# Two attention and feed-forward layers: seven-product blocks start one feature group later, and their sums are spread over plain units

## The chip, the cores and the metric

The kernel runs on one core of a Trainium2 chip. The core has five engines with queues of their own: TensorE (PE in the profile; its weight loads are listed as PEld), VectorE (DVE), ScalarE (ACT), GpSimd (POOL) and SyncE (SP, which here only issues DMA transfers). The metric is the device time of one execution in microseconds, lower is better. The time before is the median of three runs, 2001.54 us (2000.5 to 2002.94).

## The reference

The input is x with 2048 rows of 448 numbers in 32-bit float. Two layers with the same weights are applied; each is an attention stage and a feed-forward stage, both on a normalized copy of x and both added to x:

```python
x = x + _A_ref(_layernorm(x), A_wq, A_wk, A_wv, A_wo)   # 16 heads of 28, one shared key and value head
x = x + _B_ref(_layernorm(x), B_w_gate, B_w_up, B_w_down)
# and the same two lines once more

def _B_ref(x, w_gate, w_up, w_down):
    g = _silu(x @ w_gate)          # 448 x 1792
    u = x @ w_up                   # 448 x 1792
    return (g * u) @ w_down        # 1792 x 448
```

Only the feed-forward stages are touched by the change.

## The kernel before

**Precision.** Every matrix operand is split into a high part and a rest (`h` and `l` in names, by `split` on GpSimd: a rounding copy at line 139 and a subtraction at line 140), and a product is the sum of three: high by high, high by rest, rest by high.

**Tiling of the feed-forward stage.** The 2048 rows of x are four chunks of 512. The 1792 features are 14 slices of 128, here called features 0 to 13, and taken in seven groups of two (FG = 2), groups 0 to 6. The 448 inputs are three slices of 128 and one of 64; the last is held twice, in both halves of the partitions. All matrix products of the stage are issued in pairs, one on the lower 64 rows of the array and one on the upper 64 (`side_by_side`, line 338), so that two run side by side.

**Plain units.** `unit(group, chunk, n)` does one feature for one chunk: gate and up products into two of four low PSUM banks (42 products in 21 pairs), silu on ScalarE (line 1092), the product with up on VectorE (1093), rounding on ScalarE (1094), the rest on VectorE (1097). The down products of a unit (24 in 12 pairs, into four high banks) are kept in a list, `pend`, and are issued inside the next unit: one half between the two halves of its gate and up products, the other after them. Down products of both features of a group gather in the same four banks; then `accumulate` adds the four tiles to x: two on VectorE straight from PSUM (line 996), two by a staging copy on ScalarE (999) and an addition on GpSimd (1000). There are two staging buffers. `between` (line 345) reads one column of a bank on ScalarE, to keep the order of the two halves.

**Blocks of seven products.** `block(p, fc)` does one feature for two chunks (pair p is chunks 0 and 1, or 2 and 3). For the first two of the input slices, gate and up and the two chunks form a 2 by 2 by 2 product, which is done with seven products and not eight; the third and fourth slices are done as in a unit. The seven products use sums and differences: of the weights (`sums`: four on GpSimd, lines 801 to 804, and a split into the tile S of that feature), and of the inputs (`mix`, lines 788 to 793, 18 steps for each pair of chunks, into the tiles T). The sums are put together after the products on VectorE (line 852), then silu, product, rounding and rest follow as in a unit (860 to 871). A block has 39 pairs of gate and up products where two units have 42, and as many down products, which go to x after each feature (880 to 887). The stream of a block is an order written out by hand, the string ORDER: a name without a dash belongs to the newest block, with one dash to the block before, and so on. A1 to A4 and S0 to S5 are gate and up products, E1, E2, F1, F2 down products; x2 and x3, w1 and w2 are places where other jobs are put in.

**Which group is what, before.** Group 0 and group 6 are plain units, groups 1 to 5 are blocks (`mixed`, line 765): in the order of the program, two units of chunk 0 inside the attention stage, six units of group 0, twenty blocks, eight units of group 6.

**What comes ahead of the first block, before.** `rest` (line 1160 and after) loads the gate and up columns of features 2 and 3 into the one raw buffer `wr` and sums them on GpSimd, one after the other; it then gives GpSimd the first six of the 18 mixing steps for pair 0, all before the six units of group 0. The other twelve are fed to GpSimd by units, up to four each (the list `more`). The 18 mixing steps for pair 1 run on VectorE (the list `extra`, scratch tile qraw): from unit (0, 3, 0) on, four in each unit, and then in the blocks, two at x2 and three at x3. The normalized chunk 3 is turned by 16 transposes on TensorE (line 288) inside unit (0, 2, 1), from copies on GpSimd (line 249). Here (0, 3, 0) is the unit of group 0, chunk 3, first feature.

**Weights.** `weights(fc)` loads a feature's columns by DMA on SP's queue into `wr` and `wdr` (one buffer each) and splits them on GpSimd in twelve steps, into one of three sets of buffers. Features 0 to 2 come during the attention stage, feature 3 is asked for by unit (0, 3, 0) and issued in unit (0, 3, 1), and from feature 4 on blocks fetch them at w1 and w2.

**What sets the order.** The schedule is manual: each engine and SP's queue runs its instructions in the order in which the program issues them, and waits for others by semaphores.

Of the kernel before, what the change touches and what calls it, by code (L numbers as in the profile page):

```python
# [11 lines left out]
ALU = mybir.AluOpType  # L12
# [11 lines left out]
NC = S // 512  # L24
NG = H // 4
NF = F // P
FG = 2
# [6 lines left out]
@with_exitstack  # L34
def kernel(ctx: ExitStack, tc: tile.TileContext, *aps):

    nc = tc.nc  # L40
    keep = ctx.enter_context(tc.tile_pool(name="keep", bufs=1))
    fine = keep.tile([P, 16], F32, name="fine")
    nc.gpsimd.memset(fine, 1.0)
    least = keep.tile([P, 1], F32, name="least")
    whole = keep.tile([1, 1], F32, name="whole")
    forward(tc, (fine, least, whole), False, *aps)
    ok = nc.values_load(whole[0:1, 0:1].bitcast(mybir.dt.int32), skip_runtime_bounds_check_because="compared with 0 only")
    with tc.If(ok == 0, label="again"):
        forward(tc, None, True, *aps)
# [3 lines left out]
def forward(  # L53
# [14 lines left out]
    nc = tc.nc  # L68
# [57 lines left out]
    def rows3(dst, src):  # L126
        n = src.shape[1]
        nc.sync.dma_start(dst[:, 0:3], src[0:384, :].rearrange("(k p) n -> p k n", p=P))
        nc.sync.dma_start(dst[:, 3], src[384:448, :][None].to_broadcast([2, 64, n]))
# [27 lines left out]
    def columns(fc):  # L157
        fs = slice(P * fc, P * fc + P)
        r = wpool.tile([P, 4, 2, P], F32, name="wr")
        for b, src in enumerate((w_gate, w_up)):  # L160
            rows3(r[:, :, b, :], src[:, fs])
        return r

    def loaded(fc):
        r = columns(fc)
        rd = wpool.tile([P, D], F32, name="wdr")
        nc.sync.dma_start(rd, w_down[P * fc : P * fc + P, :])
        return r, rd

    def weights(fc):  # L170
        tiles, steps = parted(*loaded(fc))
        for f in steps:
            f()
        return tiles

    def parted(r, rd):
        h = wpool.tile([P, 4, 2, P], F32R, name="wgh", bufs=FG + 1)
        l = wpool.tile([P, 4, 2, P], F32R, name="wgl", bufs=FG + 1)
        dh = wpool.tile([P, D], F32R, name="wdh", bufs=FG + 1)
        dl = wpool.tile([P, D], F32R, name="wdl", bufs=FG + 1)  # L180
        steps = [lambda k=k: split(h[:, k], l[:, k], r[:, k]) for k in range(4)]
        steps += [lambda ns=ns: split(dh[:, ns], dl[:, ns], rd[:, ns]) for ns in (slice(0, 224), slice(224, D))]
        return (h, l, dh, dl), steps
# [165 lines left out]
    class Attention:  # L349
# [412 lines left out]
                        ff.left.pop(0)()  # L762

    groups = [range(f, min(f + FG, NF)) for f in range(0, NF, FG)]
    mixed = () if full else range(1, len(groups) - 1)
    HALVES = slice(0, 64), slice(64, 128)

    ORDER = (
        "A1 C21- Fc2-- Fp2-- mulA- A2 fY fX Fa0-- Fa1-- A3 fZ fW Fc3-- Fp3-- A4 s1 hhA- u2 E1- w1 w5 fE- u3 S0 "
        "hlA- x2 gY E2- Ea0- Ea1- x3 Ec2- Ep2- Ec3- Ep3- w2 S1 gX S2 gZ S3 gW S4 F1- C12 C22 silB mulB fF- S5 hhB hlB F2- silA"  # L770
    ).split()

    class FeedForward:
# [138 lines left out]
        def blocked(self, gi):  # L912

            A, B = groups[gi]
            if not self.blocks:
                one, two, *adds = self.pend
                self.pend = []
                self.blocks.append({"E1": one, "E2": two, "Ea0": adds[0], "Ec2": lambda: [f() for f in adds[1:]]})
                self.tmp = pers.tile([P, 4, 512], F32, name="xn")
            last = gi == mixed[-1]  # L920

            def fetch(fc):
                self.raw = loaded(fc)

            def part(fc, z=None):
                if not z:
                    self.W[fc], self.steps = parted(*self.raw)
                for f in self.steps[3:] if z else self.steps[: 6 if z is None else 3]:
                    f()

            def sums(fc):
                if fc // FG in mixed:
                    self.sums(fc, self.raw[0])

            jobs = [
                {"w1": [lambda: part(B)] if gi > mixed[0] else [], "w2": [lambda: fetch(A + 2)]},
                {"w1": [lambda: sums(A + 2)], "w2": [lambda: part(A + 2, 0)]},
                {"w1": [lambda: part(A + 2, 1)], "w2": [lambda: fetch(A + 3)]},
                {"w2": [lambda: sums(A + 3)]},
            ]  # L940
            for j, (p, fc) in enumerate((p, fc) for p in range(2) for fc in (A, B)):
                for n, k in (("x2", 2), ("x3", 3)):
                    jobs[j][n] = [self.extra.pop(0) for _ in range(min(k, len(self.extra)))]
                self.blocks.append(self.block(p, fc))
                self.run(jobs[j])
            if last:
                o = self.blocks[-1]
                self.blocks.append({})
                ends = [[o.pop(e + k) for k in e_.split()] for e, e_ in (("E", "1 2 a0 a1 a2 a3"), ("F", "1 2 a0 a1 a2 a3"))]
                fences = [o.pop("fE"), o.pop("fF")]  # L950
                for k in ("Ec2", "Ec3", "Ep2", "Ep3"):
                    del o[k]
                self.run({})
                part(A + 3)
                self.pend, self.late = (
                    [lambda f=f, g=g: (f[0](), g()), f[1], f[2], lambda f=f: [f_() for f_ in f[3:]]] for f, g in zip(ends, fences)
                )
# [97 lines left out]
        def unit(self, gi, c, n):  # L1055
            fs = groups[gi]
            fc = fs[n]
# [50 lines left out]
            self.pend = self.down(fs, fc, d, hh, hl)  # L1108
            if n == len(fs) - 1:
                self.pend += self.accumulate(gi, c, d)  # L1110
            for fs_, k in ((self.more, 4), (self.extra, 4)):
                for _ in range(min(k, len(fs_))):
                    fs_.pop(0)()
            if c == NC - 1 and mixed and not fc:
                self.pend.append(lambda: self.W.__setitem__(FG + 1, weights(FG + 1)))
            elif c == NC - 1 and not mixed and fc + FG + 1 < NF:
                self.pend.append(lambda: self.W.__setitem__(fc + FG + 1, weights(fc + FG + 1)))

        def close(self, c, fc, pg, sg, hh, hl, first):
# [40 lines left out]
        def rest(self, xb):  # L1160
# [15 lines left out]
                f()  # L1176
            self.soon.append([1, lambda: [f() for f in third[5:]]])
            if mixed:
                for fc in (FG, FG + 1):
                    self.sums(fc, columns(fc))  # L1180
                self.more = self.mix(0, nc.gpsimd, self.apart, lambda o, i: nc.gpsimd.tensor_scalar(o, i, 1.0, 0.0, ALU.mult, ALU.add))
                for f in self.more[:6]:
                    f()
                del self.more[:6]
            self.mid[0, 2, 1] = [lambda ks=ks: self.turned(3, ks) for ks in ((0, 1), (2, 3))]
            for gi, fs in enumerate(groups):
                if self.layer == 1 and fine is not None and gi in (0, len(groups) - 1):
# [61 lines left out]
    for c in range(1, NC):  # L1249
        fs, got = norm_steps(c)  # L1250
        n = 4 * c - 4
# [38 lines left out]
```

## Time and profile before

| | before |
|---|---|
| median of three runs | 2001.54 us |
| the profiled execution, its own time | 2000.67 us |
| its span, first to last instruction | 1998.9 us |
| TensorE busy | 1962.7 us, 98% |
| ScalarE busy | 1355.7 us, 68% |
| VectorE busy | 1069.5 us, 54% |
| GpSimd busy | 798.9 us, 40% |
| mean granted TensorE clock | 0.992 |

Times in the profile's views are microseconds from the start of the span. Layer 0's feed-forward stage runs from about 570 to 1000 us and layer 1's from about 1560 to 1999 us. A row of a timeline has start, duration, engine, line, operation, output and inputs, shapes and count; a bracket at its end gives the idle time of the engine ahead of it and who ended it. Rows of the chain have start, duration, engine, tile and line.

### The profile page before, as it was taken

The numbers are of one execution on the slowest core, as the hardware profiler recorded it, in microseconds if no ns is written. First come the engines' busy times: TensorE is split into PE (matmuls) and PEld (weight loads), VectorE is DVE, ScalarE is ACT, GpSimd is POOL, SyncE is SP. The second block draws the span as 40 slices with busy tenths as digits, with TensorE's granted clock in tenths as the row PEclk, the third lists the DMA queues.
The fourth block names the chain that finished last, engine by engine and source line by source line (L and its number), as shares of the span: only waits on it lengthen the run. The fifth ranks groups of instructions, "written<-read, shape, count | busy, mean of one in ns | idle before, by whom it ended". The sixth has DMA issues, their size and how long they took to land. (4 is left out here: it accounts for less than half of the span.)

```text
span 1998.9 us, 45604 instructions
## 1 busy us (share of the span) xinstructions
PE 1962.7 (98%) x18267; PEld 1324.4 (66%) x18267; DVE 1069.5 (54%) x1777; ACT 1355.7 (68%) x2409; POOL 798.9 (40%) x1024
## 2 busy tenths in 40 slices
PE   9999999999998899999999999999999989999998
PEld 7544545445467899999884444454454768999997
DVE  7444543545434766676564335445454347767653
ACT  4899898998953344454349998989989424544442
POOL 4212111132218677776341221111241285777640
PEclk9999999999998999999999999999999989999999
DMA  5101110211210100110131111102121110110102
GB/s 163 54 26 29 29 50 14 51 39 41 58 28 27 31 28 20 32 32 25 53 104 36 30 31 30 44 12 62 40 58 35 32 31 18 32 32 17 32 16 75
DMA packets 97632, 79.68 MB, mean 40 GB/s; under 512 B 23655, under 2 KB 80615, under 8 KB 97415
## 3 DMA queue, kind: packets, MB, share of 16 engines
q1 hardware_dynamic: 97126, 76.26, 13.7%
q8 instruction: 144, 2.36, 0.5%
q14 instruction: 74, 0.60, 0.1%
q10 hardware_dynamic: 288, 0.46, 0.1%
HBM read 57.15 MB, written 18.74 MB: 38 GB/s over the span
## 5 line engine op out<-in xcount | busy, mean ns | idle before, releaser
L662 PE MATMUL bank<-pt,vsb 128*32 128x512 f32 x4096 | 493.3, 598 | 0.3
L621 PE MATMUL bank<-qstack,keys 32*128 32x512 f32 x1536 | 484.4, 424 | 0.0
L621 PE MATMUL three<-qstack,keys 32*128 32x512 f32 x4608 | 460.1, 425 | 1.5 <-DVE vt L555 1.2
L621 PEld LDWEIGHTS three<-qstack,keys 32*128 32x128 f32 x4608 | 254.1, 182 | 295.3 <-ACT pt L634 180.3
L628 ACT ACTIVATE pt<-three 128x1536 f32<-128x1536 f32 x256 | 372.2, 1454 | 0.9 <-PE bank L662 0.5
L634 ACT ACTIVATE pt<-three 128x1536 f32<-128x1536 f32 x256 | 372.1, 1453 | 0.0
L338 PE MATMUL bank<-xh,wgh 64*128 64x512 f32 x1248 | 357.4, 396 | 7.0 <-ACT sg L861 6.6
L338 PE MATMUL bank<-wdh,h 64*128 64x448 f32 x1776 | 341.3, 366 | 9.4 <-ACT stage L999 7.8
L630 DVE COPY raw<-bank 128x512 f32<-128x512 f32 x256 | 177.2, 692 | 226.3 <-PE bank L621 224.0
L672 DVE TENSOR_TENSOR o<-bank,o 128x512 f32<-128x512 f32 x224 | 154.9, 691 | 241.0 <-PE bank L662 236.4
L338 PE MATMUL bank<-xh,wgl 64*128 64x512 f32 x924 | 281.5, 393 | 0.0
L701 POOL TENSOR_TENSOR o<-o 128x512 f32<-128x512 f32 x32 | 41.2, 1288 | 582.0 <-DMA o<-rd 542.5
L345 ACT COPY seen<-bank 128x1 f32<-128x1 f32 x820 | 105.1, 163 | 247.7 <-PE bank L338 174.2
L662 PEld LDWEIGHTS bank<-pt,vsb 128*32 128x32 f32 x4096 | 107.1, 109 | 249.8 <-issue 152.6
L338 PEld LDWEIGHTS bank<-wdh,h 64*128 64x128 f32 x1776 | 255.9, 185 | 21.3 <-ACT stage L999 8.6
L887 POOL TENSOR_TENSOR xres<-stage,xres 128x448 f32<-128x448 f32 x152 | 187.0, 1242 | 163.1 <-ACT stage L880 162.9
L338 PE MATMUL bank<-xl,wgh 64*128 64x512 f32 x816 | 245.3, 394 | 0.0
L621 PEld LDWEIGHTS bank<-qstack,keys 32*128 32x128 f32 x1536 | 243.3, 183 | 0.8 <-DVE o L672 0.6
L338 PE MATMUL bank<-wdl,h 64*128 64x448 f32 x888 | 226.4, 370 | 0.0
L852 DVE TENSOR_TENSOR xn<-bank,xn 128x512 f32<-128x512 f32 x240 | 157.8, 685 | 104.1 <-PE bank L338 84.2
L338 PEld LDWEIGHTS bank<-xh,wgh 64*128 64x128 f32 x1248 | 199.1, 186 | 19.9 <-POOL qstack L140 6.6
L633 ACT ACTIVATE pt<-bank 128x512 f32<-128x512 f32 x256 | 151.4, 592 | 59.4 <-PE bank L621 59.2
(200 smaller groups left out, 3227.2 us busy)
## 6 DMA issues: line engine op xcount, KB each, us to landing
o<-rd SPq DMA_DIRECT2D x32, 256.0 KB
qraw<-qd SPq DMA_DIRECT2D x128, 56.0 KB
qd<-stage SPq DMA_DIRECT2D x30, 224.0 KB
xt<-xn SPq DMA_DIRECT2D x28, 224.0 KB
wdr<-in_B_w_down_dram SPq DMA_DIRECT2D x28, 224.0 KB
wr<-in_B_w_gate_dram SPq DMA_DIRECT2D x32, 192.0 KB
wr<-in_B_w_up_dram SPq DMA_DIRECT2D x32, 192.0 KB
xn<-xt SPq DMA_DIRECT2D x7, 768.0 KB
```

What stands on the lines that cost most here:

```text
L338: nc.tensor.matmul(po, a, b, start=start, stop=stop, skip_group_check=True)
L345: nc.scalar.copy(seen[:, i : i + 1], po[:, 0:1])
L621: nc.tensor.matmul(three[:, j, :] if j < 3 else one, k[js, kp, ks], q[js, part, :], start=(z == 0), stop=(z == 2), tile_position=(32 * j, 0),)
L628: nc.scalar.activation(pt, three, AF.Exp, scale=SCALE)
L630: nc.vector.tensor_copy(raw, one)
L633: nc.scalar.activation(pt1, one, AF.Exp, scale=SCALE)
L634: nc.scalar.activation(pt, three, AF.Exp, scale=SCALE)
L662: nc.tensor.matmul(po[32 * j : 32 * j + 32, :], vsb[:, n % NT, :], pts[n][j], start=(n == 2 * d), stop=(n > 2 * d), skip_group_check=True,)
L672: nc.vector.tensor_tensor(acc, in_turn(po), acc, ALU.add)
L701: nc.gpsimd.tensor_tensor(rb, oraw, rb, ALU.mult)
L852: plus = lambda out, po, r: tt(by_tile(out), in_turn(po), by_tile(r), ALU.add)
L887: nc.gpsimd.tensor_tensor(r, h[e, t], r, ALU.add)
```

## The change

Blocks start with group 2 and not with group 1; group 1 becomes eight plain units in each layer. What the blocks need ahead is moved:

- The sums for the first two block features (now 4 and 5) are no longer made at the head of the stage. Their columns are loaded in units (1, 1, 0) and (1, 2, 0) and summed on GpSimd in units (1, 1, 1) and (1, 2, 1).
- No mixing step is issued ahead of the units. Each unit takes up to two steps of pair 0 (on GpSimd) and two of pair 1 (on VectorE, from unit (0, 3, 0) on) where it took four of each. With 14 units ahead of the first block both lists are empty by then, which an assertion states, and the places x2 and x3 leave the order of the block.
- Features 3, 4 and 5 are loaded by units of chunk 3, each three features ahead, where only feature 3 was.

Numerically, group 1 is now computed with eight products where it had seven.

```diff
-    mixed = () if full else range(1, len(groups) - 1)
+    mixed = () if full else range(2, len(groups) - 1)
...
-        "hlA- x2 gY E2- Ea0- Ea1- x3 Ec2- Ep2- Ec3- Ep3- w2 S1 gX S2 gZ S3 gW S4 F1- C12 C22 silB mulB fF- S5 hhB hlB F2- silA"
+        "hlA- gY E2- Ea0- Ea1- Ec2- Ep2- Ec3- Ep3- w2 S1 gX S2 gZ S3 gW S4 F1- C12 C22 silB mulB fF- S5 hhB hlB F2- silA"
...
             last = gi == mixed[-1]
+            assert not self.more and not self.extra
...
-                for n, k in (("x2", 2), ("x3", 3)):
-                    jobs[j][n] = [self.extra.pop(0) for _ in range(min(k, len(self.extra)))]
...
-            for fs_, k in ((self.more, 4), (self.extra, 4)):
-                for _ in range(min(k, len(fs_))):
+            if mixed and gi == mixed[0] - 1 and c in (1, 2):
+                if n == 0:
+                    self.raw = columns(groups[mixed[0]][c - 1])
+                else:
+                    self.sums(groups[mixed[0]][c - 1], self.raw)
+            for fs_ in (self.more, self.extra):
+                for _ in range(min(2, len(fs_))):
                     fs_.pop(0)()
-            if c == NC - 1 and mixed and not fc:
-                self.pend.append(lambda: self.W.__setitem__(FG + 1, weights(FG + 1)))
-            elif c == NC - 1 and not mixed and fc + FG + 1 < NF:
+            if c == NC - 1 and fc + FG + 1 < NF and not (mixed and fc >= FG * mixed[0] - 1):
                 self.pend.append(lambda: self.W.__setitem__(fc + FG + 1, weights(fc + FG + 1)))
...
-                for fc in (FG, FG + 1):
-                    self.sums(fc, columns(fc))
-                self.more = self.mix(0, nc.gpsimd, self.apart, lambda o, i: nc.gpsimd.tensor_scalar(o, i, 1.0, 0.0, ALU.mult, ALU.add))
-                for f in self.more[:6]:
-                    f()
-                del self.more[:6]
+                gs = nc.gpsimd
+                self.more = self.mix(0, gs, self.apart, lambda o, i: gs.tensor_scalar(o, i, 1.0, 0.0, ALU.mult, ALU.add))
```

## The prediction

> **What bounds the kernel now.** I read the page first, then the busy time by stretches, then TensorE's rows with their idle times, then the chain of waits and the timelines of the other engines around those idle times.
>
> ```profile
> span 1998.9 us, 45604 instructions
> PE   9999999999998899999999999999999989999998
> PEclk9999999999998999999999999999999989999999
> ```
>
> The span is TensorE nearly everywhere; a slice is 50 us, and the 8s of slices 13, 14 and 33 are the entries of the two feed-forward stages, where the clock dips too. The next view sums stretches; the first column is the length, then busy time and instruction count of each engine, then the granted clock.
>
> ```profile
> 593.36:711.78 118.42, 107.52 (x894) 95.83 (x894) 73.94 (x107) 44.33 (x156) 79.16 (x90) 0.94 0.09 25
> 1583.83:1701.86 118.03, 107.17 (x894) 94.23 (x894) 72.86 (x108) 44.30 (x156) 79.37 (x90) 0.94 0.09 25
> 1701.86:1927.78 225.92, 225.92 (x2022) 219.45 (x2019) 156.09 (x227) 109.14 (x402) 157.74 (x197) 1.00 0.10 28
> 1591.22:1598.52 7.30, 7.30 (x69) 6.63 (x67) 2.46 (x5) 2.77 (x10) 4.83 (x7) 1.00 0.22 62
> 1964.78:1979.37 14.59, 14.59 (x135) 13.01 (x133) 4.36 (x7) 4.42 (x17) 1.25 (x1) 1.00 0.17 64
> ```
>
> The first two rows run, in each layer, from the second chunk's first unit of group 0 to the first block of group 2: six plain units, the transposes of chunk 3, and the four blocks of group 1. The third row is the sixteen blocks of groups 2 to 5: TensorE never idle, 225.92 / 16 = 14.12 us a block. The last two are one plain unit of group 0 and two of group 6: 7.30 us a unit in both places, with ScalarE, VectorE and GpSimd busy less than 70% of it. So in steady work two units cost 14.60 against 14.12 for the block that does the same; and the entry stretch, which at these prices would take 6 x 7.30 + 2.0 + 4 x 14.12 - 2.5 = 99.8 us (the 2.0 and 2.5 are explained below), takes 118. Some 18 us per layer are lost there. Where:
>
> ```profile
> 1613.89 0.74 PE L338 MATMUL bank<-wdh,h 64*128 64x448 f32 x1 [3.96 <-ACT stage L999]
> 1619.24 1.12 PE L288 MATMUL bank<-ident,xn 128*128 128x128 f32 x4 [1.70 <-POOL xn L249]
> 1646.75 0.49 PE L338 MATMUL bank<-xh,kdiag 64*128 64x512 f32 x1 [1.57 <-DVE xn L852]
> 1657.52 0.76 PE L338 MATMUL bank<-xh,wgh 64*128 64x512 f32 x1 [3.05 <-ACT sg L861]
> 656.54 0.50 PE L338 MATMUL bank<-xh,kdiag 64*128 64x512 f32 x1 [2.22 <-DVE xn L852]
> 668.58 0.46 PE L338 MATMUL bank<-xh,wgh 64*128 64x512 f32 x1 [2.78 <-ACT sg L861]
> ```
>
> Four idle times in layer 1 (two in unit (group 0, chunk 2, second half), two in the first block), and the latter two again in layer 0. Each is followed by a slow clock:
>
> ```profile
> 1612.92:1623.16 10.24, 7.57 (x33) 0.50 0.01 2
> 1657.29:1660.70 3.41, 3.18 (x16) 0.50 0.00 0
> 653.77:657.18 3.41, 1.19 (x12) 1.00 0.42 125
> 657.18:660.60 3.42, 3.42 (x20) 0.50 0.34 96
> 664.01:667.43 3.42, 1.78 (x15) 1.00 0.00 0
> ```
>
> The clock is granted in steps of 3.41 us. In layer 0 a step with TensorE busy 1.19 us (the 2.22 us idle) was followed by one at 0.50; the step busy 1.78 us, further on, was not. Half clock loses half its busy time: (7.57 + 3.18) / 2 = 5.4 us in layer 1. What the idle times wait for:
>
> ```profile
> ACT stage L999 <- POOL xres L1000: 7.1, 2, 6.5
> 1595.22 4.36 DMA wr<-in_B_w_up_dram
> 1612.19 2.17 POOL xres L1000 x2
> ```
>
> These are a row of the waits and two of the chain. GpSimd does the sums of two features' weights (the second after a 4.36 us load) and six mixing steps before it may add chunk 0's staged tiles (L1000, at 1612.19). ScalarE cannot stage chunk 1 before that, so its banks stay full and TensorE's down products wait 3.96 us; the copies for chunk 3's transposes (L249) are behind the same queue, 1.70 us.
>
> **The change, part by part.**
>
> *Blocks to units.* Group 1's four blocks a layer become eight units: 8 x 7.30 = 58.4 for 4 x 14.12 = 56.5, a cost of 1.9 us a layer on TensorE, which nothing hides. The first block lacks its predecessor's two last down products wherever it stands; those move with it.
>
> ```profile
> 1608.44 1.09 PE L288 MATMUL bank<-ident,xn 128*128 128x128 f32 x8
> 1609.46 0.47 PE L338 MATMUL bank<-wdh,h 64*128 64x448 f32 x1
> 1683.78 0.50 PE L338 MATMUL bank<-wdh,h 64*128 64x448 f32 x2
> 1684.81 0.50 PE L338 MATMUL bank<-wdh,h 64*128 64x448 f32 x2
> ```
>
> From these: eight transposes take 1.02 us, sixteen 2.0; one half of the down products takes 1.23 (1683.78 to a sixth pair from 1684.81), two 2.5.
>
> *Sums and first mixing leave the head of the stage.* In the new order GpSimd's queue starts with chunk 0's adds; the mixing is fed two steps a unit behind them, and the sums come in group 1. The 3.96 and 1.70 us waits and the 10.24 us of half clock go. Nothing else is late there: a unit's GpSimd work is two steps (1.37 us each by the row below) and, every second unit, two adds (2.2 us), 7.7 of 14.6 us.
>
> ```profile
> L791 POOL TENSOR_TENSOR apart<-apart,xl 128x512 f32<-128x512 f32 x4 | 5.5, 1366 | 0.3
> 1592.10 0.96 ACT L999 COPY stage<-bank 128x448 f32<-128x448 f32 x2
> 1637.20 0.86 POOL L139 TENSOR_SCALAR wgh<-wr 128x256 fp32r<-128x256 f32 x1
> 1643.67 0.82 POOL L139 TENSOR_SCALAR wdh<-wdr 128x224 fp32r<-128x224 f32 x1
> 1646.41 0.66 POOL L140 TENSOR_TENSOR wdl<-wdr,wdh 128x224 fp32r<-128x224 f32 x1
> ```
>
> *Feature 3's weights are needed sooner*: in the second unit of group 1, two units (14.6 us) after unit (0, 3, 1) starts, not a block later. Their five loads on SP's queue no longer stand behind the sums' loads, so they land early. GpSimd's adds end 3.7 us into that unit (staged from 0.9 us in, 1592.10 less 1591.22, 0.96 us of copies, two adds), two steps take it to 6.4, the gate and up splits take 6.5 (1637.20 to 1643.67): ready at 12.9, 1.7 us ahead. Cost nothing; with every step 30% longer, some 2 us late, which is the upper bound.
>
> *Two new loads with their sums* (features 4 and 5, in units (1, 1) and (1, 2)) wait on SP for the one raw buffer, behind feature 4's splits; what queues behind them on SP are only feature 5's loads, not due before the second block. On GpSimd, by the same prices, counted from the start of (0, 3, 1), feature 3's twelve splits end at 16.3 us, feature 4's at 31.2 (two steps, two adds and twelve splits later), and after four more steps the staged tiles of chunk 0 of group 1 are added by 39; the next staging needs their buffers at 6 x 7.30 + 0.9 = 44.7. With some 5.7 us of cover at these prices, the dearest in the rows: cost nothing.
>
> *Mixing for the second pair, on VectorE*, goes from four steps a unit plus five a block to two a unit, and is done before the first block.
>
> ```profile
> 1592.23 0.69 DVE L1097 TENSOR_TENSOR h<-sg,h 128x512 fp32r<-128x512 f32 x1 [0.16 <-ACT h L1094]
> 1592.84 0.62 DVE L996 TENSOR_TENSOR xres<-bank,xres 128x448 f32<-128x448 f32 x1
> 1593.76 0.38 PE L338 MATMUL bank<-wdh,h 64*128 64x448 f32 x2
> 1641.23 1.06 DVE L1097 TENSOR_TENSOR h<-sg,h 128x512 fp32r<-128x512 f32 x1 [0.69 <-ACT h L1094]
> 1636.25 1.54 DVE L790 TENSOR_TENSOR qraw<-qraw,xl 128x512 f32<-128x512 f32 x1
> 1652.46 0.39 PE L338 MATMUL bank<-keys,wgh 64*128 64x512 f32 x1
> 1653.73 1.27 DVE L852 TENSOR_TENSOR xn<-bank,xn 128x512 f32<-128x512 f32 x2
> 1654.08 0.39 PE L338 MATMUL bank<-xh,wgh 64*128 64x512 f32 x1
> 1684.03 1.29 DVE L852 TENSOR_TENSOR xn<-bank,xn 128x512 f32<-128x512 f32 x2 [2.35 <-PE bank L338]
> ```
>
> At a chunk's end VectorE's add frees a bank at 1593.46 (1592.84 + 0.62), 0.30 us before TensorE's next down product. While GpSimd was splitting, the subtraction ahead of it took 1.06 us for 0.69: 0.37 longer, 0.07 past the cover. Some six chunk ends a layer have GpSimd busy: 0.4 us a layer; bounds 0 and six times 0.9 (a step that waits out a whole GpSimd step of 1.2 us).
>
> [...]
>
> In the first block, S0's second product waited because VectorE still mixed (1.57 and 2.22 us); with no mixing there, it goes. The second wait stays in part. The chain is: sums of banks y and z (L852), silu, product, rounding, silu of bank x, and only then may the next block's A1 write x; in later blocks two down products cover it, in the first there are none. S5 begins at 1652.46 and L852 could start 0.25 us after (as 1684.03 after 1683.78), at 1652.71; it started at 1653.73, 1.02 late behind mixing. From S5's last issue (1654.08 + 0.23) to A1 (1657.52) are 3.2 us; 2.2 remain, 1.8 if the product too is short without company: I take 2.0 a layer. That idle is between the 1.63 us of the step that kept its clock (3.42 less 1.78) and the 2.22 that lost it, if it falls in one step at all; I take no half clock, and 1.7 us a layer for the upper end.
>
> [...]
>
> **The sum.** New entry stretch, per layer: 14 x 7.30 + 2.0 - 2.5 + 2.0 + 0.4 = 104.1 us, after which sixteen blocks follow as before (225.92). Gain 118.42 - 104.1 = 14.3 in layer 0 and 118.03 - 104.1 = 13.9 in layer 1, 28.2 together. The profiled execution took 2000.67 us around its span of 1998.9, within 0.05% of the median 2001.54, so I leave it: 2000.67 - 28.2 = 1972.5 us. No change means within 0.2% (4 us), about what a measurement of this kernel can tell.
>
> **Rivals.**
> - *The first block keeps all its waits* because another VectorE or ScalarE delay fills the place of the mixing. For it: later blocks run the same chain with only 0.2 us to spare. Against: their rows show no wait above 0.4. Price: layer 0 2.2 + 0.9 + 1.7, layer 1 1.6 + 1.2 + 1.6, 9.2 us: 1982.
> - *GpSimd and VectorE collide.* Both mix in the same units. For: the step at 1636.25 took 1.54 us. Against: the slack of units (VectorE 2.46 of 7.30). Price by the upper bound, 5 us a layer: 1982 to 1987 with late weights.
> - *One staging trip a layer:* the adds fall behind feature 4's splits or the sums, and the wait of 3.96 us with 10.24 us of half clock returns in group 1: 4.0 + 5.1 = 9.1 us a layer: 1991. Needs GpSimd some 6 us later than reckoned, and 4 more for the whole wait.
> - *Slower:* two such trips a layer, one at feature 4's splits and one at a sum whose load is late: 36.4 us against 28.2: 2009. It decides only when GpSimd is 10 us late at both places, its steps a third longer than the dearest rows.
> - *The spreading only moves the queue* and gains what the units cost: 2000.
>
> **Chances.** Forecast 0.70 (its own range 1967 to 1980: no wait at all in the first block, down; half clock in both layers and half the collision bound, up). First block 0.10, collision 0.09, one trip 0.05, slower 0.04, nothing 0.02. The range 1967 to 1985 holds the forecast, the first-block case and part of the collision. Faster 0.94, same 0.02, slower 0.04.
>
> **What would show it.** Right: no TensorE idle and clock 1.00 from the first unit of the stage to the first block, which starts 14 units (about 104 us) after unit (0, 1, 0); one idle of 1.5 to 2.2 us per layer before the second block's A1; L249 done before the transposes. Wrong: ScalarE's L999 waiting for GpSimd's L1000 again, TensorE waiting for a split (L139, L140) at unit (1, 0, 1), VectorE's L996 freeing banks late in group 1, or half clock after the first block.

## The result and the profile after

| | before | after |
|---|---|---|
| median, us | 2002.13 (2000.5 to 2002.94) | 1977.34 (1976.81 to 1978.09) |
| ratio of the medians, 95% interval | | 0.9877 (0.986 to 0.9895) |
| the profiled execution, its own time | 2000.67 | 1978.09 |
| its span | 1998.9 | 1976.4 |
| mean granted clock | 0.992 | 0.997 |

The median of before now includes runs made beside those of after. The change gains 24.8 us. 1972.5 us was predicted; 4.8 us more was measured, which is inside the range.

The page of after has these slices, where those of before were quoted in the prediction:

```profile
PE   9999999999999999999999999999999999999998
PEclk9999999999999999999999999999999999999999
```

The 8s at the two stage entries are gone, in both rows. The busy time by stretches has the same columns as in the prediction. The first two rows run from the second chunk's first unit of group 0 to the first block, now group 2; the next two from there to the last block's silu of bank x (line 861):

```profile
593.98:699.07 105.09, 105.09 (x942) 95.77 (x943) 57.44 (x81) 38.24 (x135) 69.82 (x79) 1.00 0.09 26
1572.17:1677.76 105.59, 105.31 (x943) 90.78 (x942) 57.99 (x82) 38.31 (x136) 70.33 (x80) 1.00 0.09 25
699.07:924.70 225.63, 223.51 (x1985) 216.56 (x1984) 149.74 (x219) 106.25 (x392) 150.24 (x187) 0.99 0.10 28
1677.76:1903.83 226.07, 223.95 (x1984) 214.06 (x1986) 150.73 (x218) 106.11 (x391) 149.28 (x187) 0.99 0.10 28
```

The same sixteen blocks in the kernel before, from the first one of group 2 to the same silu:

```profile
711.78:936.77 224.99, 224.53 (x2010) 219.32 (x2009) 154.63 (x225) 108.62 (x400) 158.53 (x197) 1.00 0.10 28
1701.86:1926.45 224.59, 224.59 (x2010) 218.55 (x2009) 154.87 (x225) 107.96 (x399) 157.69 (x196) 1.00 0.10 28
```

From the first of these points to the last, layer 0 took 118.42 + 224.99 = 343.41 us before and 105.09 + 225.63 = 330.72 after; layer 1 took 118.03 + 224.59 = 342.62 before and 105.59 + 226.07 = 331.66 after. The gains are 12.7 and 11.0 us. The forecast had 14.3 and 13.9. Of the 23.7 us, 22.5 remain in the span; 0.6 went because layer 0's stage began that much later (593.98 for 593.36), the other 0.5 elsewhere.

What is left is one wait a layer. TensorE's timeline of after has these two rows, the only idle times over 0.3 us in the four stretches:

```profile
712.90 0.47 PE L338 MATMUL bank<-xh,wgh 64*128 64x512 f32 x1 [2.12 <-ACT sg L861]
1691.79 0.46 PE L338 MATMUL bank<-xh,wgh 64*128 64x512 f32 x1 [2.12 <-ACT sg L861]
```

Here are the steps of the clock around them: in each layer the step that holds the idle time, and the one after it.

```profile
709.94:713.35 3.41, 1.29 (x12) 0.89 (x10) 2.62 (x4) 1.75 (x3) 2.62 (x3) 1.00 0.00 0
713.35:716.76 3.41, 3.41 (x20) 3.26 (x18) 1.22 (x2) 0.64 (x4) 0.00 (x0) 0.50 0.02 5
1689.57:1692.98 3.41, 1.29 (x10) 0.89 (x11) 2.62 (x4) 1.26 (x3) 1.97 (x2) 1.00 0.00 0
1692.98:1696.39 3.41, 3.41 (x18) 2.69 (x20) 0.68 (x2) 1.21 (x6) 0.00 (x0) 0.50 0.00 0
```

This is the second block's A1 waiting for the first block's silu of bank x, as forecast, with the half clock that the forecast left out.

### The profile page after: what moved, and what is told of

Same layout as the page of the kernel before. It is cut to its first block, busy times and chain, and to the rows that moved or that the text cites. A ratio compares the mean times of both kernels' runs of the same rounds, so it can differ in the third digit from the quotient of the medians.

```text
span 1976.4 us, 45477 instructions
## 1 busy us (share of the span) xinstructions
PE 1957.4 (99%) x18315; PEld 1314.6 (67%) x18315; DVE 1030.3 (52%) x1713; ACT 1339.5 (68%) x2353; POOL 763.8 (39%) x984
## 5 line engine op out<-in xcount | busy, mean ns | idle before, releaser
L338 PE MATMUL bank<-xh,wgh 64*128 64x512 f32 x1344 | 372.9, 392 | 4.7 <-ACT sg L861 4.2
L338 PE MATMUL bank<-wdh,h 64*128 64x448 f32 x1776 | 335.1, 364 | 1.7 <-DVE xres L885 0.9
L338 PE MATMUL bank<-xh,wgl 64*128 64x512 f32 x1020 | 297.7, 390 | 0.0
L345 ACT COPY seen<-bank 128x1 f32<-128x1 f32 x788 | 100.1, 163 | 244.7 <-PE bank L338 183.0
L338 PE MATMUL bank<-xl,wgh 64*128 64x512 f32 x912 | 261.8, 390 | 0.0
L338 PEld LDWEIGHTS bank<-wdh,h 64*128 64x128 f32 x1776 | 247.5, 184 | 14.6 <-DVE xres L885 2.6
L338 PE MATMUL bank<-wdl,h 64*128 64x448 f32 x888 | 222.3, 367 | 0.0
L338 PEld LDWEIGHTS bank<-xh,wgh 64*128 64x128 f32 x1344 | 207.4, 185 | 19.3 <-POOL qstack L140 5.0
L887 POOL TENSOR_TENSOR xres<-stage,xres 128x448 f32<-128x448 f32 x120 | 146.4, 1232 | 138.2 <-ACT stage L880 138.0
L852 DVE TENSOR_TENSOR xn<-bank,xn 128x512 f32<-128x512 f32 x192 | 126.4, 686 | 95.5 <-PE bank L338 74.7
```

Of the source, the lines that this page charges most:

```text
L338: nc.tensor.matmul(po, a, b, start=start, stop=stop, skip_group_check=True)
L345: nc.scalar.copy(seen[:, i : i + 1], po[:, 0:1])
L852: plus = lambda out, po, r: tt(by_tile(out), in_turn(po), by_tile(r), ALU.add)
L887: nc.gpsimd.tensor_tensor(r, h[e, t], r, ALU.add)
```

## The experiments

The theory is the prediction's: the entry was slow because GpSimd's and VectorE's extra work stood ahead of steps that TensorE needed, and each piece of it can be moved to where it has cover. Its main rival is that the gain comes from one part alone, or from starting the blocks later, and that the spreading is nothing. All ratios are to the kernel before, on the same chip; the medians of before on the chips differ by some 0.1%, so small differences between two experiments are read from the traces and not from the medians.

| | median, us | ratio (95%) |
|---|---|---|
| after | 1977.34 | 0.9877 (0.986 to 0.9895) |
| 1 sums and six mixing steps first | 1988.48 | 0.9938 (0.9921 to 0.9955) |
| 2 sums first | 1975.05 | 0.9866 (0.9849 to 0.9882) |
| 3 six mixing steps first | 1976.18 | 0.9869 (0.9853 to 0.9886) |
| 4 VectorE mixes late and in the block | 1984.11 | 0.9912 (0.9896 to 0.9929) |
| 5 down products a place later | 1971.11 | 0.9852 (0.9839 to 0.9866) |
| 6 TensorE kept busy in the wait | 1973.84 | 0.9868 (0.9852 to 0.9883) |
| 7 blocks from group 3 | 1978.23 | 0.9888 (0.9873 to 0.9903) |
| 8 no blocks | 1982.3 | 0.9912 (0.9897 to 0.9928) |
| 9 GpSimd 17.6 us late | 1991.69 | 0.9956 (0.994 to 0.9972) |
| 10 spread, blocks from group 1 | 1993.72 | 0.9968 (0.9954 to 0.9981) |
| 11 10 and 5 | 1995.45 | 0.9973 (0.9963 to 0.9983) |
| 12 spread again, with room, and 5 | 1979.87 | 0.9888 (0.9872 to 0.9905) |

### 1 to 3: the head of GpSimd's queue

Three kernels put work back ahead of the units, in place of where the change has it: both parts, only the sums, only the six mixing steps. Blocks still start with group 2. Run 1:

```diff
-            if mixed and gi == mixed[0] - 1 and c in (1, 2):
+            if False:
...
                 gs = nc.gpsimd
+                for fc in groups[mixed[0]]:
+                    self.sums(fc, columns(fc))
                 self.more = self.mix(0, gs, self.apart, ...)
+                for f in self.more[:6]:
+                    f()
+                del self.more[:6]
```

Run 2 has the first two of the three parts, run 3 the third alone.

> The changed kernel, with the old head put back: both features' sums, then six mixing steps, on GpSimd ahead of the units; blocks still begin with group 2. My theory (GpSimd's queue at the head makes the first two waits and their half clock): both waits return in unit (0, 2, 1), 4.0 + 1.7 us idle and some 7.6 / 2 us of half clock, 9.5 us a layer, 1996 us. Rival (those waits hung on the blocks starting one group earlier): stays at 1977.

> As the run before it, but only the sums go ahead of the units, not the mixing. My theory: the sums end near 20 us after unit (0, 1, 0) starts, the adds then need 2.2, and the banks are wanted at 25.6: within the cover, 1977 to 1979 us. Rival (the sums with their 4.36 us load are the whole cause): 9.5 us a layer, 1996.

> Only the six mixing steps go ahead of the units, the sums stay in group 1. My theory: 8 us of GpSimd's time, within the cover, 1977 us. Rival (the mixing is the cause): up to 1996.

TensorE's timeline of run 1:

```profile
622.03 0.47 PE L338 MATMUL bank<-wdh,h 64*128 64x448 f32 x1 [3.52 <-ACT stage L998]
1606.14 0.74 PE L338 MATMUL bank<-wdh,h 64*128 64x448 f32 x1 [3.83 <-ACT stage L998]
```

Its busy time around the first of these:

```profile
622.86:629.69 6.83, 6.62 (x31) 0.50 0.01 2
```

With both parts at the head the staging wait is back in both layers (3.5 and 3.8 us, 3.96 before), and each is followed by 6.83 us of half clock. The stretch from the third unit's silu to the last unit's grew from 97.7 to 105.1 us in layer 0. The wait for L249 did not return. Units still feed only two steps: in layer 0 GpSimd's timeline has two of them, 2.5 us, between chunk 0's adds and L249's copies, and the one of before has four, 4.6 us. So the time is 11 us over after, where the expectation was 19 over.

With either part alone that stretch is 97.69 and 97.77 us, as in after: no staging wait, no half clock before the blocks. Neither the sums nor the mixing alone was the cause; only the two together are longer than the cover. That decides against the rival of one guilty part.

Runs 2 and 3 and after are also the same kernel at the second block's wait, 2.12 or 2.13 us in each, and still differ. In the profiled executions after loses the clock in both layers, run 3 in layer 0 alone, run 2 in none. TensorE's timeline and clock of run 2 there:

```profile
711.68 0.47 PE L338 MATMUL bank<-xh,wgh 64*128 64x512 f32 x1 [2.13 <-ACT sg L861]
```

```profile
708.05:711.46 3.41, 1.50 (x14) 1.00 0.00 0
711.46:714.88 3.42, 3.20 (x25) 1.00 0.02 5
```

The same idle time begins 1.50 us into its step, where after's began 0.84 us into it; 0.2 us of it fall into the next step, and the clock stays. So a part of what separates these three kernels is where the wait happens to fall, and not what was moved: the four executions of after all have a mean clock of 0.997, those of run 3 lie between 0.997 and 1.000.

What a half clock costs is in the time from the first block's silu of bank x to the second's, here in layer 1. Of after:

```profile
1691.05 0.59 ACT L861 ACTIVATE sg<-bank 128x512 f32<-128x512 f32 x1
1706.71 0.60 ACT L861 ACTIVATE sg<-bank 128x512 f32<-128x512 f32 x1
```

Of run 2:

```profile
1687.75 0.59 ACT L861 ACTIVATE sg<-bank 128x512 f32<-128x512 f32 x1
1701.84 0.60 ACT L861 ACTIVATE sg<-bank 128x512 f32<-128x512 f32 x1
```

15.66 us with it, 14.09 without: 1.57 us. In layer 0 the two are 15.37 and 14.10, 1.27 us.

### 4: VectorE's mixing back in the first block

```diff
-        "hlA- gY E2- Ea0- Ea1- Ec2- ...
+        "hlA- x2 gY E2- Ea0- Ea1- x3 Ec2- ...
...
+                for n, k in (("x2", 2), ("x3", 3)):
+                    jobs[j][n] = [self.extra.pop(0) for _ in range(min(k, len(self.extra)))]
...
-            for fs_ in (self.more, self.extra):
-                for _ in range(min(2, len(fs_))):
+            for fs_, k in ((self.more, 2), (self.extra, 4)):
+                for _ in range(min(k, len(fs_))):
...
-                        if mixed and (gi, c, n) == (0, 3, 0):
+                        if mixed and (gi, c, n) == (mixed[0] - 1, 3, 0):
```

> The changed kernel, with VectorE's mixing for the second pair begun only in unit (1, 3, 0), four steps a unit, and the rest in the first two blocks as before. My theory: S0's wait of 1.6 to 2.2 us returns and A1's wait grows by 1.0 us, 2.6 to 3.2 us a layer: 1983 us. Rival (the first block's waits are only those of an empty pipe): 1977.

TensorE's timeline in layer 0:

```profile
703.48 0.50 PE L338 MATMUL bank<-xh,qstack 64*128 64x512 f32 x1 [2.22 <-DVE xn L852]
714.25 0.46 PE L338 MATMUL bank<-xh,wgh 64*128 64x512 f32 x1 [3.05 <-ACT sg L861]
```

VectorE's timeline ahead of the first row:

```profile
699.86 1.12 DVE L788 TENSOR_TENSOR qraw<-xh 128x512 f32<-128x512 f32 x1
701.01 0.75 DVE L790 TENSOR_TENSOR qraw<-qraw,xl 128x512 f32<-128x512 f32 x1
701.79 1.03 DVE L791 TENSOR_TENSOR qraw<-qraw,xl 128x512 f32<-128x512 f32 x1
702.75 2.07 DVE L852 TENSOR_TENSOR xn<-bank,xn 128x512 f32<-128x512 f32 x3
```

Both waits of before return: 2.22 and 1.53 us at S0 (2.22 and 1.57 before), 3.05 and 3.03 at A1 (2.78 and 3.05 before). VectorE is mixing without a pause until it comes to line 852, which S0 waits for. Moving this mixing ahead is worth 6.8 us of the 24.8 by the medians (1984.11 less 1977.34), where 6 were expected. The spans of the profiled executions differ by only 4.3 us (1980.7 and 1976.4); there run 4 has one half clock in the stages, in layer 1, and after has two, so the clock hides a part of the price.

### 5: cover for the second block's wait

The down products of the last unit are given to the first block at E1 and E2. Here the second half is issued at F1 and F2 of the second block's stream, where a block's own second half goes:

```diff
-                self.blocks.append({"E1": one, "E2": two, "Ea0": adds[0], "Ec2": lambda: [f() for f in adds[1:]]})
+                self.blocks.append({"E1": one, "F1": two, "Fa0": lambda: [f() for f in adds]})
```

> The changed kernel; only the last unit's second half of down products moves in the first block, from between S0 and S1 (the place E2) to between S4 and S5 (F1), and the four adds behind it. My theory: the wait before the second block's A1 falls from 2.1 us by 1.2, under what halves the clock, so 1.2 + 1.7 us a layer are won, and some 0.4 lost before S1: 1972 us. Rival (the half clock after it has another cause): only 0.8 us a layer, 1976. Other rival: S1 waits as much as A1 gains, 1977.

TensorE's timeline at the two waits:

```profile
710.92 0.46 PE L338 MATMUL bank<-xh,wgh 64*128 64x512 f32 x1 [0.78 <-ACT sg L861]
1686.78 0.46 PE L338 MATMUL bank<-xh,wgh 64*128 64x512 f32 x1 [0.80 <-ACT sg L861]
```

2.12 became 0.78 and 0.80, a fall of 1.33 us for the 1.23 us that one half of the down products takes, and no step in the stages lost its clock. The ratio, 0.9852, is the lowest of all, and the span 1970.2 us against 1976.4. This version beats the kernel before with certainty, and after by 5 us in the ratios, whose intervals still overlap.

### 6: the clock or the wait

Fourteen transposes into a bank that is free are issued ahead of the second block; they do nothing but keep TensorE busy in the same wait.

```diff
                 self.blocks.append(self.block(p, fc))
+                if gi == mixed[0] and j == 1:
+                    for _ in range(14):
+                        nc.tensor.transpose(banks[4][:, 0:P], ident, ident)
                 self.run(jobs[j])
```

> The changed kernel with 14 idle transposes (1.8 us) put into the wait before the second block's A1, into a bank that nobody reads. My theory (the idle step of 3.41 us makes the half clock): the wait stays, the half clock goes, 1.7 us a layer won: 1974 us. Rival (the clock answers to something else, such as the mix of work): 1977 or more.

TensorE's timeline:

```profile
710.11 1.75 PE L946 MATMUL bank<-ident 128*128 128x128 f32 x14
712.28 0.46 PE L338 MATMUL bank<-xh,wgh 64*128 64x512 f32 x1 [0.43 <-ACT sg L861]
```

The silu is waited for as long as before (1.75 and 0.43 make 2.18), yet no step of the stages lost its clock, and the first two blocks' silus are 14.09 us apart in both layers (15.37 and 15.66 in after). The median is 3.5 us lower for the 2.8 that these differences give. So the half clock comes from TensorE's idleness, and its price can be had back while the wait stays.

### 7 and 8: how many groups are blocks

```diff
-    mixed = () if full else range(2, len(groups) - 1)
+    mixed = () if full else range(3, len(groups) - 1)
```

Run 8 has `mixed = ()` in the same place.

> Blocks from group 3 on, all else as in the changed kernel. My theory: one more group a layer at the unit's price, 58.4 for 56.5 us, nothing else moves: 1.9 us a layer, 1981 us. Rival (waits on GpSimd or VectorE in group 1 still cost, and ease when spread thinner): 1977 to 1979.

> No blocks at all: every group is plain units, with eight products each, and no sums and no mixing. My theory: four groups a layer cost 1.9 us each, 15.2 us in all, and the entry into the blocks no longer costs (2.3 us of wait, 1.7 of half clock and some 1.3 of small waits a layer, 10.6 us): 1982 us. Rival (the blocks save what their product count says, three pairs of 0.23 us each in 16 blocks a layer, 22 us): 1989.

In run 7, 22 units from the third on take 156.03 us by their silus where after's 14 take 97.69: eight units for 58.34. Four blocks took 4 x 14.08 = 56.33. The price of a group, 2.0 us a layer (1.9 in the prediction), holds. The time rose by less than these 4.0 us, 2.2 by the ratios where 3.8 were expected, since of the two half clocks one was left, in layer 0 from 769.6 us.

Without blocks the kernel takes 1982.3 us, 17.9 under the kernel before on the same chip (2000.22). As set up there, the scheme of seven products cost more at its entry than its twenty blocks a layer saved. In after it is worth some 5 us by the medians and 7 by the ratios; in run 5, on the same chip, 11.2.

### 9: how much cover GpSimd has

Fourteen subtractions into a tile that is written anew later stand on GpSimd after the unit (1, 0, 0), ahead of the adds of (1, 0).

```diff
+            if mixed and (gi, c, n) == (mixed[0] - 1, 0, 0):
+                for _ in range(14):
+                    nc.gpsimd.tensor_tensor(self.S[0][1], self.apart, self.apart, ALU.subtract)
```

> The changed kernel with 14 idle subtractions (some 18 us) on GpSimd in unit (1, 0, 0), into a buffer that is not in use yet. By the changed kernel's trace the adds of group 1's chunk 0 end 8 us ahead of the next staging. My theory: 10 us late, ScalarE's staging waits, TensorE stands some 8 us and then runs at half clock for two or three steps, 12 us a layer: 2001 us. Rival (GpSimd in group 1 has no hold on TensorE): 1977.

GpSimd's timeline, and in the second fence ScalarE's waits in layer 0 and in the third TensorE's timeline:

```profile
660.17 17.61 POOL L1112 TENSOR_TENSOR qstack<-apart 128x512 fp32r<-128x512 f32 x14
```

```profile
ACT stage L998 <- POOL xres L999: 8.6, 2, 8.0
```

```profile
684.57 0.74 PE L338 MATMUL bank<-wdh,h 64*128 64x448 f32 x1 [6.67 <-ACT stage L998]
```

Of 17.6 us of delay 8.0 reach ScalarE's staging and 6.7 TensorE (6.67 in layer 1 too), with 6.83 us of half clock around it in each layer. So the adds had 17.6 - 8.0 = 9.6 us of cover where the prediction had 5.7. Of this some was made up on the way, since two adds took 2.23 us here and 2.74 to 2.76 in after, whose own rows give 7.9 us (below). The mechanism of the staging rival is real, with its price: 14 us for both layers together, where 24 were expected (a part of the difference: the second block's wait kept its clock here). The rival of this run, that GpSimd's lateness costs nothing, is out.

### 10 to 12: the spreading without the later start

Run 10 spreads the work as the change does, but over the units of group 0 alone, and blocks start with group 1. Each unit of group 0 takes what is given for it of the 18 steps, VectorE four a unit with x2 and x3 back in ORDER as in run 4, and the sums stand in units (0, 1, 1) and (0, 2, 1):

```diff
-    mixed = () if full else range(2, len(groups) - 1)
+    mixed = () if full else range(1, len(groups) - 1)
...
+            if mixed and gi == 0:
+                for _ in range({(1, 0): 5, (2, 0): 5, (3, 0): 4, (3, 1): 4}.get((c, n), 0)):
+                    self.more.pop(0)()
+                for _ in range(min(4, len(self.extra))):
+                    self.extra.pop(0)()
```

In this kernel and in run 11 feature 3's sums go through the scratch tile on GpSimd while a mixing step's part sum is still in it, so that some values of the tiles T are not those of the reference; the instructions and their sizes are the same.

> Blocks from group 1 on as before the change, but nothing at the head of GpSimd's queue: its sums for features 2 and 3 go into units (0, 1, 1) and (0, 2, 1), its mixing in whole items of four or five steps into units (0, 1, 0), (0, 2, 0), (0, 3, 0) and (0, 3, 1); VectorE mixes as before, from (0, 3, 0) into the first two blocks. My theory: the first two waits go (9.5 us a layer of the 18 lost before), the first block's stay, no units are added: 2002 less 19, 1983 us. Rival (six units do not hold GpSimd's work, 44 us of steps in 44 us): the adds are late again, above 1990.

> The run before it with the last unit's second half of down products moved to F1 in the first block. My theory: A1's wait falls by 1.2 us and its half clock may go, 2.5 to 3 us a layer: 1978 us, still above the same move with blocks from group 2 (1971). Rival (VectorE's mixing in the block sets that wait, whatever TensorE does in it): 1983.

TensorE's timeline of run 10, and GpSimd's:

```profile
655.23 0.79 PE L338 MATMUL bank<-keys,wgh 64*128 64x512 f32 x1 [5.01 <-POOL keys L1186]
```

```profile
650.43 0.97 POOL L140 TENSOR_TENSOR wdl<-wdr,wdh 128x224 fp32r<-128x224 f32 x1
651.36 1.70 POOL L788 TENSOR_TENSOR apart<-xh,apart 128x512 f32<-128x512 f32 x1
653.14 1.32 POOL L791 TENSOR_TENSOR apart<-apart,xl 128x512 f32<-128x512 f32 x1
654.55 0.62 POOL L1186 TENSOR_SCALAR keys<-apart 128x512 fp32r<-128x512 f32 x1
```

The last four mixing steps of pair 0 came behind feature 3's twelve splits, and the first block reached for the tile that they make 5.0 us early. Two half clocks of 3.41 and 6.83 us (10.24 in layer 1) stand around it. Run 10 was expected at 1983 and gave 1993.72: a miss for the theory, for a reason that the rival had named: six units are not room enough in that order. Run 11 was to gain 5 us by the edit of run 5 and gained nothing; its wait for the same tile is 6.27 us long, and what run 5's edit saves is waited there.

Run 12 gives GpSimd the same work in an order that fits: columns in (0, 1, 0) and (0, 1, 1), sums in (0, 1, 1) and (0, 2, 0), the steps in (1, 0), (2, 0), (2, 1) and (3, 0), and run 5's edit.

```diff
+                if (c, n) in ((1, 1), (2, 0)):
+                    self.sums(groups[1][c - 1], self.raw)
+                if (c, n) in ((1, 0), (1, 1)):
+                    self.raw = columns(groups[1][n])
+                for _ in range({(1, 0): 5, (2, 0): 5, (2, 1): 4, (3, 0): 4}.get((c, n), 0)):
+                    self.more.pop(0)()
```

> Blocks from group 1 on, spread in a better order than the last two: GpSimd's sums in units (0, 1, 1) and (0, 2, 0), its mixing items in (0, 1, 0), (0, 2, 0), (0, 2, 1) and (0, 3, 0), all ahead of feature 3's splits; down products at F1 as in the run with the move alone, which has blocks from group 2 (1971). My theory: GpSimd fits now, four blocks a layer save 2.0 us, but VectorE must mix inside the first block, 1.9 us of wait at S0 and 1.0 more at A1 a layer: 1971 - 4 + 6 = 1973 us, with a half clock or two up to 1976. Rival (six units are too few for GpSimd in any order): 1985 or more. Other rival (only the queue's order mattered, the later start nothing): 1967.

TensorE's timeline, and VectorE's ahead of the first row:

```profile
647.95 0.50 PE L338 MATMUL bank<-xh,kdiag 64*128 64x512 f32 x1 [2.94 <-DVE xn L852]
1621.37 0.49 PE L338 MATMUL bank<-xh,wgh 64*128 64x512 f32 x1 [1.88 <-DVE sg L1094]
```

```profile
642.77 1.78 DVE L793 TENSOR_TENSOR mixed<-qraw,mixed 128x512 fp32r<-128x512 f32 x1
644.59 0.77 DVE L788 TENSOR_TENSOR qraw<-xh 128x512 f32<-128x512 f32 x1
645.40 1.09 DVE L790 TENSOR_TENSOR qraw<-qraw,xl 128x512 f32<-128x512 f32 x1
646.53 0.77 DVE L791 TENSOR_TENSOR qraw<-qraw,xl 128x512 f32<-128x512 f32 x1
```

TensorE waits for GpSimd no more, but for VectorE: 2.94 us at S0 in layer 0 behind four mixing steps without a pause, 1.88 us at the block's entry in layer 1 with a half clock behind it. 1979.87 us was measured for 1973 expected, 1976 with half clocks. Some 2 us of the difference are the chip's, whose kernel before took 2002.17 us; the rest was not traced. Run 5, which is the same with blocks from group 2, has 1971.11, 7 us less by the ratios. So the four blocks that group 1 gives up cost 4 us (run 7's price), and the eight units that take their place give VectorE's mixing room that group 0 does not have. The later start is not the price of the spreading; it is a part of it. Whether another order of VectorE's steps would fit into group 0's units was not tried, and stays open.

## Why the prediction was right, and by how much it was not

*What bounded the kernel.* Right. Putting the work back at the head (run 1) and into the block (run 4) brings back three of the four waits that the prediction had read from before, at the same places, with the same lengths to 0.3 us (layer 0's staging wait was 3.82 us before). The fourth, L249's 1.70 us a layer, and the third step of half clock beside it came back in neither: no run put the feed of four mixing steps a unit back, so their cause is read from the traces alone. Nor was the later start run by itself, with both loads put back at once.

*Blocks to units, 1.9 us a layer.* Right: 2.0 by run 7.

*Sums and first mixing leave the head.* Right as a sum, too simple as a cause. The waits and 10.24 us of half clock went; but runs 2 and 3 show that either part of the work could have stayed at the head.

*Feature 3's weights.* Right: forecast 1.7 us ahead of the unit that needs them. GpSimd's timeline of after has the last gate and up split done by 1624.1 (1623.36 + 0.74), and that unit's first product started at 1626.0, 1.9 us later. The same view has the adds of chunk 0 of group 1, and L249's copies:

```profile
1589.03 1.50 POOL L249 COPY xn<-xn 128x64 f32<-128x64 f32 x4 [3.01 <-DVE xn L247]
1623.36 0.74 POOL L140 TENSOR_TENSOR wgl<-wr,wgh 128x256 fp32r<-128x256 f32 x1
1645.68 2.74 POOL L999 TENSOR_TENSOR xres<-stage,xres 128x448 f32<-128x448 f32 x2
```

TensorE's timeline of after at that unit:

```profile
1626.00 0.39 PE L338 MATMUL bank<-xh,wgh 64*128 64x512 f32 x1
```

ScalarE's timeline of after has the next staging copies, which need the buffers that these adds free:

```profile
1656.29 0.96 ACT L998 COPY stage<-bank 128x448 f32<-128x448 f32 x2
```

*Cover of 5.7 us for the staging.* Right in sign, too small: the adds end at 1648.42 and the copies start at 1656.29, 7.9 us later; 9.6 us by run 9. The prediction had taken the dearest rows for every step. L249's copies end at 1590.53, 6.2 us ahead of the transposes, which start at 1596.77.

*Collisions of VectorE and GpSimd, 0.4 us a layer.* Too dear, and the reason for it was wrong. The prediction took the 0.37 us by which VectorE's row at 1641.23 was longer for the price of a collision at every chunk end. GpSimd's timeline of before has what ran beside that row:

```profile
1641.02 0.73 POOL L140 TENSOR_TENSOR wgl<-wr,wgh 128x256 fp32r<-128x256 f32 x1
```

VectorE's subtraction had begun inside this instruction, which ended at 1641.75, and ended itself at 1642.29, 0.54 us later. In after's two stages 95 VectorE instructions with both inputs in SBUF, that is with none in a PSUM bank (lines 788 to 793, 862, 871 and 1096), began at least 0.1 us before the end of a GpSimd instruction that was running. Every one of them ended 0.53 to 0.58 us after that end, and the longest took 1.83 us. Undisturbed they take 0.69 us. The 122 with an input in a bank (L852, L1092) that began beside GpSimd in the same way took at most 0.69 us, as they do alone. So the 0.37 us was no fixed price: in all of these rows VectorE's end followed GpSimd's, however much was left of the latter's instruction. What kept it cheap is room: VectorE is busy 57 of 105 us in this stretch, and of all the units from (0, 3, 1) on one alone, in layer 1, is late, by 0.03 us. The collision rival at 5 us a layer is out.

*Units and transposes.* Fourteen units and the transposes, with the 0.4 us of collisions, were to take 14 x 7.30 + 2.0 + 0.4 = 104.6 us; they took 105.09 and 105.59. By their silus the units are 7.29 us apart, but the unit with the transposes takes 9.73 us and the one after it 7.74 or 7.75. That is 0.9 us a layer over the 2.0 us that the prediction had for the transposes, in matmuls that start about 0.1 us late, which the view counts as busy. The collisions that did not come give 0.4 of it back. In layer 1 another 0.4 us are lost at the first block, 0.28 of them as idle time, waiting for the last unit's product (L1092), which VectorE started as soon as its silu was done.

*The first block.* S0's wait went, as forecast. The wait at A1 is 2.12 us in both layers for a forecast of 2.0.

*No half clock.* This is the term that was mis-sized. "I take no half clock, and 1.7 us a layer for the upper end": it came in both layers, at 1.27 and 1.57 us. The prediction had put the idle time between 1.63 us, which kept the clock, and 2.22, which lost it, and took the hopeful side of an open interval. It named the condition, "if it falls in one step at all", and gave it no price; the last section shows that this condition decided it.

The shortfall in the stages is 28.2 - 23.65 = 4.55 us: half clock 2.84, units and transposes 1.5, A1 0.24, and what is left, under 0.1, is the difference of rests of 0.3 us of each sign. The rest of the 5.6 us between 1972.5 and the profiled 1978.09 is the 0.6 us by which layer 0's stage began later, and 0.4 elsewhere. None of this belongs to a rival: the first block did not keep its waits, no staging trip came back, and the slower case needed GpSimd 10 us late at two places, where run 9 shows about 10 us of cover at one of them.

## What to carry to other kernels

Work that an engine is given early is free only up to what stands behind it in its queue: add up the queue to the first step that somebody waits for, since two loads of which each is harmless (97.7 us with either) can cost 7 us a layer together. At a pipeline's entry, look for what the first iteration lacks as cover and move finished work there: one half of the down products, a place later, was worth some 5 us and needed one line. And price a faster scheme with its entry: twenty blocks of seven products a layer, as first set up, were 18 us slower than none.

## What the hardware showed that was not expected

An idle time of the same 2.12 us cost a half clock or not by where it fell in the clock's steps. Over the profiled executions of all kernels with blocks from group 2 or 3 in which this wait stood unchanged (after, 1, 2, 3, 7, 9), it halved the clock in four layers of twelve. All of it fell into one step in those four; in the other eight the step's share was 1.91 us or less. From all the waits, the border is not sharp. Run 2 kept its clock with 1.50 us busy in the step (shown above). Run 12 lost it with 1.53 us (the first fence), and run 10 with 1.77 (the second), at a step that holds two waits of its first block in layer 1; run 11 lost it at the same place with 1.77 as well:

```profile
1618.92:1622.33 3.41, 1.53 (x14) 1.00 0.00 0
1622.33:1625.74 3.41, 3.41 (x19) 0.50 0.00 0
```

```profile
1625.66:1629.07 3.41, 1.77 (x13) 1.00 0.00 0
1629.07:1632.48 3.41, 3.41 (x20) 0.50 0.00 0
```

So between 1.64 and 1.91 us idle of 3.41 both came, and what else decides there is open. The steps of run 2 are reckoned back from its last half clock, at the end of the span, in steps of 3.413 us, so its 1.50 is less certain than the 1.53. Run 4's longer wait of 3.05 us in layer 0 was split over two steps, 1.76 us busy in the first and 2.02 in the second, and did not halve the clock either:

```profile
709.44:712.85 3.41, 1.76 (x15) 1.00 0.00 0
712.85:716.27 3.42, 2.02 (x15) 1.00 0.02 5
```

The length of a step is read from before's 10.24 us at half clock in the prediction's fences, three steps of 3.413. The half clocks of one execution start whole steps apart: in before 44.37 us, 13 steps, lie between 1612.92 and 1657.29, and in after 979.63 us, 287 steps, between its two. An idle time of 2.12 us was enough in after, where one step held it, and 3.05 us in two steps were not in run 4.

The other surprise is VectorE beside GpSimd (above): 95 times of 95, an instruction with both inputs in SBUF ended 0.53 to 0.58 us after the end of what GpSimd was running.
